# VectorE takes the square, the cast and the relu of the last feed-forward items from ScalarE

## The chip, the cores and the metric

One core of one Trainium2 chip runs the whole program. The metric is device time in microseconds (us) of one execution. Engines go by short names: PE is TensorE (PEld its weight loads), DVE is VectorE, ACT is ScalarE, POOL is GpSimd and SP is SyncE, which issues the DMAs.

## The reference

Three layers follow one another: a chunked attention (batch 4, 8 heads, 768 positions, head size 64), a soft mixture of experts, and a squared-relu feed-forward layer. The change touches only the last, whose reference is

```
h = x @ w_in                  # 3072 x 512 by 512 x 2048
r = np.maximum(h, 0.0)
g = s * (r * r) + b
out = g @ w_out               # 3072 x 2048 by 2048 x 512
```

Since `x` is itself a mixture of 32 expert outputs, the kernel computes `h` from a packed pair of small matrices and never builds `x`.

## The kernel before, in words

The first 180 us or so hold the attention and the experts. The rest is one loop over **items** (variable `n`, last loop of the kernel, from line 979 on in the profile's numbering). An item is one block of 384 tokens (`b`, 8 of them) with one slice of 128 hidden units (`f`, 16 of them), 128 items in all. The order is written out in `runs` and `items`: blocks 0 and 1 alternate for the first half of the slices (items 0 to 15), blocks 2 and 3 alternate (16 to 47), then blocks 4 to 7 follow one at a time (48 to 63, 64 to 79, 80 to 95, 96 to 111), and the second halves of blocks 0 and 1 end the program (112 to 119, 120 to 127).

One item `n` passes through these steps:

- `emit_h` (L823, PE): one matmul of 384 columns into a PSUM buffer `s`, of which there are two. I call its start T_n.
- `emit_relu` (L829, ACT), `emit_sq` (L833, ACT) and `emit_ghi` (L837, ACT): relu out of PSUM into `r`, square into `r2`, and a rounding cast into `ghi`. `r` and `r2` have two buffers each and both are printed as `r` in the profile, `ghi` and `glo` have five.
- `emit_g` (L840, DVE): the split `glo = r2 - ghi`, what the cast lost. It is issued one round later.
- `emit_o` (L875, PE), three rounds later (LA = 3): three matmuls of 512 columns of `ghi` against `w_hi`, then three of `glo` against `w_hi`. `emit_o2` (L887), one round after that: three of `ghi` against `w_lo`. All gather in three PSUM banks of the block.

When a block's last slice is done, four rounds after its `emit_h`, three **evictions** (L897, DVE) scale the three banks, add the bias and hand them to a store. With the blocks above they come in rounds 67, 83, 99, 115, 123 and 131, ahead of that round's other work on DVE.

Beside that, rounds 48 to 63 sum the weights on DVE for the bias, `colsum` makes the bias in round 64 (L850 on PE, L851 on DVE), and rounds 65 to 76 each issue one `add_bias` (L862) on POOL: a `tensor_tensor` of 128x512 with both sources in SBUF, twelve in all. They wait for the bias and for sums evicted long before, so POOL runs them back to back. The first six feed stores, the other six the evictions of rounds 123 and 131.

The whole section runs under a manual schedule: each engine takes its instructions in the order in which the program writes them, and waits only where it reads or overwrites what another wrote.

Of the kernel before, what the change touches and what calls it, by code (L numbers as in the profile page):

```python
# [14 lines left out]
ALU = mybir.AluOpType  # L15
# [19 lines left out]
def kernel(  # L35
# [11 lines left out]
    nc = tc.nc  # L47
# [11 lines left out]
    NF = w_out.shape[0] * 2  # L59
# [57 lines left out]
    with tc.manual_schedule():  # L117
# [624 lines left out]
        LA = 3  # L742
# [5 lines left out]
        def tiles(name, n, w, dt=F32):  # L748
            return [g_p.tile([128, w], dt, name=f"{name}{i}") for i in range(n)]
# [3 lines left out]
        r_g, r2_g = (tiles(x, 2, UT) for x in ("r", "r2"))  # L753
        ghi_g, glo_g = tiles("ghi", LA + 2, UT, F32R), tiles("glo", LA + 2, UT, F32R)
# [8 lines left out]
        items, place = [], {}  # L763
# [5 lines left out]
        h_t, o_t = {}, {}  # L769

        def stage_a(k):
            key = cq.get(k)
            if key:
                if key[0] == "i":
                    w = wi_src(key[1], key[2])
                else:
                    w = wt[raw_of[key]].rearrange("p (f d t) -> p f d t", f=2, t=2)[:, key[1] % 2]
                cv_act(key, k // 2 % 2, w)
# [39 lines left out]
        def emit_h(n):  # L818
            if n >= len(items):
                return  # L820
            (b, _, _), f = items[n]
            hq = psum("s", [128, UT])
            nc.tensor.matmul(out=hq, lhsT=mpack[:, 128 * f:128 * f + 128], rhs=cpack[:, b * UT:(b + 1) * UT],  # L823
                             start=True, stop=True)
            h_t[n] = hq

        def emit_relu(n):
            if n < len(items):
                nc.scalar.activation(out=r_g[n % 2], in_=h_t.pop(n), func=AF.Relu)  # L829

        def emit_sq(n):
            if n < len(items):
                nc.scalar.activation(out=r2_g[n % 2], in_=r_g[n % 2], func=AF.Square)  # L833

        def emit_ghi(n):
            if n < len(items):
                nc.scalar.copy(out=ghi_g[n % (LA + 2)], in_=r2_g[n % 2])  # L837

        def emit_g(n):
            nc.vector.tensor_tensor(out=glo_g[n % (LA + 2)], in0=r2_g[n % 2], in1=ghi_g[n % (LA + 2)].bitcast(F32),  # L840
                                    op=ALU.subtract)

        def wsum_add(i):
            if 0 < i < 2 * NF:
                a = w_hi[0].bitcast(F32) if i == 1 else wsum
                nc.vector.tensor_tensor(out=wsum, in0=a, in1=(w_hi, w_lo)[i % 2][i // 2].bitcast(F32), op=ALU.add)

        def colsum():
            c = psum("s", [128, DM])
            nc.tensor.matmul(out=c, lhsT=ones, rhs=wsum, start=True, stop=True)  # L850
            nc.vector.tensor_scalar(out=bias, in0=c, scalar1=sbt[:, 1:2], scalar2=None, op0=ALU.mult)  # L851
# [7 lines left out]
        def add_bias(i):  # L859
            j, t = divmod(i, NTU)  # L860
            os_ = os_early(j, t) if j < 2 else part[j - 2][t]
            nc.gpsimd.tensor_tensor(out=os_, in0=os_, in1=bias, op=ALU.add)  # L862
            if j < 2:
                store(2 + j, t, os_)

        def emit_o(n, parts=(0, 1)):
            r_, f = items[n]
            ghi, glo = ghi_g[n % (LA + 2)], glo_g[n % (LA + 2)]
            if f == r_[1] and 0 in parts:
                o_t[r_] = [psum(("pt", "x", "xt", "lp", "g", "g")[3 * place[r_] + t], [128, DM]) for t in range(NTU)]  # L870
            if n == len(items) - 1:
                return
            for gt in [(ghi, glo)[x] for x in parts]:
                for t in range(NTU):
                    nc.tensor.matmul(out=o_t[r_][t], lhsT=gt[:, 128 * t:128 * t + 128], rhs=w_hi[f],  # L875
                                     start=(f == r_[1] and gt is ghi), stop=False)

        def emit_o2(n):
            r_, f = items[n]
            b, f0, f1 = r_  # L880
            ghi, glo = ghi_g[n % (LA + 2)], glo_g[n % (LA + 2)]
            for t in range(NTU):
                o = o_t[r_][t]
                if n == len(items) - 1:
                    for gt in (ghi, glo):
                        nc.tensor.matmul(out=o, lhsT=gt[:, 128 * t:128 * t + 128], rhs=w_hi[f], start=False, stop=False)
                nc.tensor.matmul(out=o, lhsT=ghi[:, 128 * t:128 * t + 128], rhs=w_lo[f], start=False, stop=(f == f1 - 1))  # L887
                if f == f1 - 1:
                    if b < 4 and f0 == 0:
                        to = part[b][t] if b < 2 else os_early(b - 2, t)  # L890
                        if t == 1:
                            nc.scalar.activation(out=to, in_=o, func=AF.Copy, scale=sbt[:, 0:1])
                        else:
                            nc.vector.tensor_scalar(out=to, in0=o, scalar1=sbt[:, 0:1], scalar2=None, op0=ALU.mult)
                    else:
                        os_ = os_g[t]
                        nc.vector.scalar_tensor_tensor(out=os_, in0=o, scalar=sbt[:, 0:1], in1=part[b][t] if f0 else bias,  # L897
                                                       op0=ALU.mult, op1=ALU.add)
                        store(b, t, os_)
# [7 lines left out]
        def act(n):  # L907
            emit_relu(n)
            emit_sq(n)
            emit_ghi(n)  # L910
# [5 lines left out]
        def sums(n):  # L916
            if n in M_AT:
                emit_m(M_AT.index(n) + 1)
            if n - 1 in M_AT:
                emit_m2(M_AT.index(n - 1) + 1)  # L920

        def convert(n):
            stage_d(n, 1)
            stage_w(n)
            stages(n, 2, 3)
            stages(n - 1, 4, 5)
            stage_d(n + 1, 0)
# [7 lines left out]
        for k in range(2):  # L935
# [3 lines left out]
                  in_=sot[:, k:k + 1, :, 0:4].to_broadcast([128, 4, 4, 4]))  # L939
# [39 lines left out]
        for n in range(LA + 1, len(items) + LA + 1):  # L979
            if n > 7:  # L980
                emit_h(n)
            m = n - LA - 1
            ends = 0 <= m and items[m][1] == items[m][0][2] - 1
            late = m + 1 < len(items) and m + 1 == 2 * HF + 1
            if ends or late:
                emit_o2(m)
            if n == 2 * HF + 3:
                convert(n - 1)
            if 1 < m + 1 < len(items):
                emit_o(m + 1)  # L990
            if m > 1 and not ends and not late:
                emit_o2(m)
            if LA + 1 < n <= 7:
                emit_h(n)
            if n == 6:
                nc.vector.tensor_copy(out=soTb, in_=soT4[:, :, 0, :])
            if n <= 7:
                sums(n)
            emit_relu(n)
            emit_sq(n)  # L1000
            stage_a(n + 1)
            emit_ghi(n)
            if n > 7:
                sums(n)
            if LA + 1 < n <= len(items):
                emit_g(n - 1)

            if n != 2 * HF + 2:
                convert(n)
            if 48 <= n < 64:  # L1010
                for i in (2 * n - 96, 2 * n - 95):
                    wsum_add(i)
            if n == 64:
                colsum()
            if 65 <= n < 77:
                add_bias(n - 65)
            while n != 2 * HF + 2 and wnext[0] < len(order) and last_use.get(order[wnext[0] - NRG], -1) <= n:
                load_w(1)
# [72 lines left out]
```

## Time and profile before

| | before |
|---|---|
| median of 3 runs | 471.82 us (471.47 to 473.12) |
| the profiled execution | 471.86 us |
| its span, first to last instruction | 469.7 us |
| PE busy | 451.3 us (96%) |
| DVE busy | 290.2 us (62%) |
| ACT busy | 308.1 us (66%) |
| POOL busy | 84.2 us (18%) |
| mean granted TensorE clock | 0.991 |

The profiled execution is the one that the trace shows; 2.2 us of its time lie around the span. Busy shares are means over the whole program, so a stage is read by the view that cuts the trace into stretches. In a timeline row the first number is the start in us from the span's start and the second the length; a length in a group's row is a mean in ns.

### The profile page before, as it was taken

To read this page: it belongs to the slowest core of one execution; us is meant where nothing else is said; L and a number is where in the kernel's file an instruction comes from. 1 tells how busy PE (TensorE), PEld (TensorE's weight loads), DVE (VectorE), ACT (ScalarE), POOL (GpSimd) and SP (SyncE) were. 2 spreads that over 40 slices of the span, in tenths; PEclk is the share of its full clock that TensorE was granted. 3 is DMA by queue.
4 is the path that set the end of the run, shared out by engine and by line. 5 is a ranking of instruction groups with operands and counts; after the bars stand their busy time and mean duration, and the time that the engine had idled before them with its cause. 6 is when DMAs were issued, how large, how long until landed. Compare 5 with 4: busy or idle time off the path is not lost.

```text
span 469.7 us, 10190 instructions
## 1 busy us (share of the span) xinstructions
PE 451.3 (96%) x3960; PEld 341.5 (73%) x3960; DVE 290.2 (62%) x653; ACT 308.1 (66%) x635; POOL 84.2 (18%) x154
## 2 busy tenths in 40 slices
PE   5899999999999989999999999999999999999996
PEld 4666667565555467888787888888888888888885
DVE  6678888886465768977374988966523223224232
ACT  4466666666225469988686987666666666666660
POOL 6576556551000000000000000008600000000000
PEclk9799999999999999999999999999999999999999
DMA  8999999999999953425222000004001001001011
GB/s 299 388 391 408 405 399 405 407 387 355 422 412 401 414 216 109 163 89 180 89 91 90 2 0 0 1 0 190 13 0 69 0 1 68 0 1 67 1 67 67
DMA packets 20575, 83.03 MB, mean 177 GB/s; under 512 B 2736, under 2 KB 2864, under 8 KB 14640
## 3 DMA queue, kind: packets, MB, share of 16 engines
q1 hardware_dynamic: 20528, 82.39, 45.2%
q8 instruction: 31, 0.51, 0.4%
q14 instruction: 16, 0.13, 0.1%
HBM read 76.09 MB, written 6.29 MB: 175 GB/s over the span
## 4 chain that ended last, share of the span: by engine, by line
PE 77%; DMA 10%; DVE 7%; ACT 2%; SPq 2%; issue 1%; POOL 0%; DVEq 0%; POOLq 0%; ACTq 0%
PE g L875 12%; PE x L875 6%; PE xt L875 6%; PE pt L875 6%; PE lp L875 6%; PE g L887 6%; DMA seg<-in_w_dram 5%; PE s L823 5%; PE s L627 3%; PE pt L887 3%; PE lp L887 3%; PE x L887 3%; PE xt L887 3%; DMA vals<-in_vm_dram 3%; PE x L324 3%; PE s L284 3%
## 5 line engine op out<-in xcount | busy, mean ns | idle before, releaser
L840 DVE TENSOR_TENSOR glo<-r,ghi 128x384 fp32r<-128x384 f32 x128 | 76.7, 603 | 83.0 <-ACT ghi L837 82.9
L829 ACT ACTIVATE r<-s 128x384 f32<-128x384 f32 x128 | 62.8, 491 | 53.8 <-PE s L823 53.3
L833 ACT ACTIVATE r<-r 128x384 f32<-128x384 f32 x128 | 67.3, 526 | 7.3 <-DVE glo L840 3.0
L837 ACT CAST ghi<-r 128x384 fp32r<-128x384 f32 x128 | 65.4, 511 | 3.4
L823 PE MATMUL s<-cpack,mpack 128*128 128x384 f32 x128 | 44.1, 347 | 0.2 <-DVE mpack L816 0.2
L300 ACT ACTIVATE seg<-seg 128x384 f32<-128x384 f32 x32 | 28.8, 899 | 19.1 <-DVE seg L311 15.6
L875 PE MATMUL g<-whi,ghi 128*128 128x512 f32 x126 | 39.8, 396 | 0.3 <-DVE mpack L816 0.3
L887 PE MATMUL g<-wlo,ghi 128*128 128x512 f32 x128 | 39.6, 389 | 0.0
L875 PE MATMUL g<-whi,glo 128*128 128x512 f32 x126 | 39.3, 393 | 0.0
L862 POOL TENSOR_TENSOR keys<-keys,bias 128x512 f32<-128x512 f32 x6 | 8.4, 1428 | 161.7 <-DVE bias L851 161.7
L262 POOL TENSOR_SCALAR keys<-keys 64x416 f32<-64x416 f32 x63 | 33.6, 534 | 12.5 <-DMA keys<-in_kq_dram 7.4
L284 PE MATMUL s<-keys 128*32 128x128 f32 x768 | 29.6, 286 | 5.8 <-POOL keys L266 4.2
L324 PE MATMUL x<-vals,seg 128*32 128x128 f32 x744 | 27.8, 280 | 2.5 <-DMA vals<-in_vm_dram 1.0
L324 PEld LDWEIGHTS x<-vals,seg 128*32 128x32 f32 x744 | 20.3, 111 | 13.2 <-DVE seg L308 5.7
L823 PEld LDWEIGHTS s<-cpack,mpack 128*128 128x128 f32 x128 | 23.9, 188 | 7.2 <-issue 1.5
L887 PEld LDWEIGHTS g<-wlo,ghi 128*128 128x128 f32 x128 | 24.0, 188 | 5.1
L875 PEld LDWEIGHTS g<-whi,glo 128*128 128x128 f32 x126 | 23.6, 188 | 5.5
L284 PEld LDWEIGHTS s<-keys 128*32 128x32 f32 x768 | 19.1, 112 | 11.6 <-POOL keys L266 6.2
L318 ACT COPY seg<-pt 128x384 f32<-128x384 f32 x32 | 15.2, 476 | 18.1 <-PE pt L316 17.2
L875 PEld LDWEIGHTS g<-whi,ghi 128*128 128x128 f32 x126 | 23.7, 188 | 4.0 <-DVE mpack L816 0.8
L875 PE MATMUL xt<-whi,ghi 128*128 128x512 f32 x64 | 25.4, 397 | 0.0
L875 PE MATMUL pt<-whi,ghi 128*128 128x512 f32 x64 | 25.2, 394 | 0.0
(250 smaller groups left out, 965.3 us busy)
## 6 DMA issues: line engine op xcount, KB each, us to landing
seg<-in_w_dram SPq DMA_DIRECT2D x27, 1024.0 KB, 8.8
keys<-in_kq_dram SPq DMA_DIRECT2D x32, 396.0 KB, 7.4
vals<-in_vm_dram SPq DMA_DIRECT2D x64, 192.0 KB, 6.6
keys<-in_w_in_dram SPq DMA_DIRECT2D x5, 1024.0 KB, 5.1
keys<-in_w_out_dram SPq DMA_DIRECT2D x5, 1024.0 KB, 4.9
out_dram<-os SPq DMA_DIRECT2D x18, 256.0 KB, 2.0
vals<-in_w_in_dram SPq DMA_DIRECT2D x3, 1024.0 KB, 6.7
vals<-in_w_out_dram SPq DMA_DIRECT2D x3, 1024.0 KB, 4.8
```

The lines of the kernel that those rows point to most:

```text
L262: (nc.vector if h and u == 0 else nc.gpsimd).tensor_scalar(out=stream(kz[rows, h], 0, CH), in0=k[rows, UT * h:UT * h + (NCU + 1) * CH].rea ...
L284: nc.tensor.matmul(out=o, lhsT=qt[:, 32 * c:32 * c + 32], rhs=kz[:, :, at:at + WIN], start=True, stop=not (first or last))
L300: nc.scalar.activation(out=p_r[u], in_=sm_r[u].rearrange("p t h (a r) -> p t r (h a)", a=2), func=AF.Exp, scale=scale)
L318: nc.scalar.copy(out=pts_r[u], in_=pt)
L324: nc.tensor.matmul(out=xp[32 * r:32 * r + 32, t], lhsT=pts_r[u][:, 32 * c:32 * c + 32], rhs=vbuf[u // 2 % 2][:, u % 2, :, 64 * c:64 * c + ...
L823: nc.tensor.matmul(out=hq, lhsT=mpack[:, 128 * f:128 * f + 128], rhs=cpack[:, b * UT:(b + 1) * UT], start=True, stop=True)
L829: nc.scalar.activation(out=r_g[n % 2], in_=h_t.pop(n), func=AF.Relu)
L833: nc.scalar.activation(out=r2_g[n % 2], in_=r_g[n % 2], func=AF.Square)
L837: nc.scalar.copy(out=ghi_g[n % (LA + 2)], in_=r2_g[n % 2])
L840: nc.vector.tensor_tensor(out=glo_g[n % (LA + 2)], in0=r2_g[n % 2], in1=ghi_g[n % (LA + 2)].bitcast(F32), op=ALU.subtract)
L875: nc.tensor.matmul(out=o_t[r_][t], lhsT=gt[:, 128 * t:128 * t + 128], rhs=w_hi[f], start=(f == r_[1] and gt is ghi), stop=False)
L887: nc.tensor.matmul(out=o, lhsT=ghi[:, 128 * t:128 * t + 128], rhs=w_lo[f], start=False, stop=(f == f1 - 1))
```

## The change

From item 66 on (`DSQ = 4 * NF + 2`, with NF = 16) the square, the cast and the split are issued together on DVE, right after the relu, and ACT does none of them. From item 78 on (`DRELU = 5 * NF - 2`) the relu is a DVE instruction too, a `tensor_scalar` maximum out of PSUM, and ACT has no instruction left. `emit_g` of these items therefore moves one round earlier. The PE, POOL and SP programs are the same, instruction for instruction.

```
+        DSQ, DRELU = 4 * NF + 2, 5 * NF - 2
+
         def emit_relu(n):
-            if n < len(items):
+            if n >= len(items):
+                return
+            if n < DRELU:
                 nc.scalar.activation(out=r_g[n % 2], in_=h_t.pop(n), func=AF.Relu)
+            else:
+                nc.vector.tensor_scalar(out=r_g[n % 2], in0=h_t.pop(n), scalar1=0.0, scalar2=None, op0=ALU.max)
+            if n >= DSQ:
+                nc.vector.tensor_tensor(out=r2_g[n % 2], in0=r_g[n % 2], in1=r_g[n % 2], op=ALU.mult)
+                nc.vector.tensor_copy(out=ghi_g[n % (LA + 2)], in_=r2_g[n % 2])
+                emit_g(n)
 
         def emit_sq(n):
-            if n < len(items):
+            if n < DSQ:
                 nc.scalar.activation(out=r2_g[n % 2], in_=r_g[n % 2], func=AF.Square)
 
         def emit_ghi(n):
-            if n < len(items):
+            if n < DSQ:
                 nc.scalar.copy(out=ghi_g[n % (LA + 2)], in_=r2_g[n % 2])
@@
-            if LA + 1 < n <= len(items):
+            if LA + 1 < n <= DSQ:
                 emit_g(n - 1)
```

DVE's row from the bias of round 64 to the split of item 67, before (L851 is the bias, L840 a split, L897 an eviction):

```order
L851 TENSOR_SCALAR bias_2666<-s,cstt 128x512
L840 TENSOR_TENSOR glo_2664<-r_2653,ghi_2659 128x384
L840 TENSOR_TENSOR glo_2660<-r_2654,ghi_2655 128x384
L897 SCALAR_TENSOR_TENSOR os_2647<-pt,cstt,bias_2666 128x512
L897 SCALAR_TENSOR_TENSOR os_2648<-x,cstt,bias_2666 128x512
L897 SCALAR_TENSOR_TENSOR os_2649<-xt,cstt,bias_2666 128x512
L840 TENSOR_TENSOR glo_2661<-r_2653,ghi_2656 128x384
L840 TENSOR_TENSOR glo_2662<-r_2654,ghi_2657 128x384
```

The same stretch after the change (L861 is the bias, L837 the square, L838 the cast, L850 the split, L907 an eviction):

```order
L861 TENSOR_SCALAR bias_2666<-s,cstt 128x512
L850 TENSOR_TENSOR glo_2664<-r_2653,ghi_2659 128x384
L837 TENSOR_TENSOR r_2653<-r_2651 128x384
L838 CAST ghi_2656<-r_2653 128x384
L850 TENSOR_TENSOR glo_2661<-r_2653,ghi_2656 128x384
L850 TENSOR_TENSOR glo_2660<-r_2654,ghi_2655 128x384
L907 SCALAR_TENSOR_TENSOR os_2647<-pt,cstt,bias_2666 128x512
L907 SCALAR_TENSOR_TENSOR os_2648<-x,cstt,bias_2666 128x512
L907 SCALAR_TENSOR_TENSOR os_2649<-xt,cstt,bias_2666 128x512
L837 TENSOR_TENSOR r_2654<-r_2652 128x384
L838 CAST ghi_2657<-r_2654 128x384
L850 TENSOR_TENSOR glo_2662<-r_2654,ghi_2657 128x384
```

The split of item 65 (into `glo_2660`) now stands behind three instructions of item 66, and square, cast and split of item 67 stand behind the three evictions.

DVE's row at items 77 and 78 after the change (L835 is the relu):

```order
L837 TENSOR_TENSOR r_2654<-r_2652 128x384
L838 CAST ghi_2657<-r_2654 128x384
L850 TENSOR_TENSOR glo_2662<-r_2654,ghi_2657 128x384
L835 TENSOR_SCALAR r_2651<-s 128x384
L837 TENSOR_TENSOR r_2653<-r_2651 128x384
L838 CAST ghi_2658<-r_2653 128x384
L850 TENSOR_TENSOR glo_2663<-r_2653,ghi_2658 128x384
```

From here on DVE has four instructions for an item where it had one.

## Rows read from the trace of the kernel before

**Rows 1.** The page, busy time of PE: us, share of the span, instructions.

```profile
PE 451.3 (96%) x3960; PEld 341.5 (73%) x3960; DVE 290.2 (62%) x653; ACT 308.1 (66%) x635; POOL 84.2 (18%) x154
```

**Rows 2.** Stretches: length, then busy us and instructions of each engine, clock, DMA.

```profile
340.00:380.00 40.00, 40.00 (x181) 33.23 (x180) 11.81 (x21) 27.39 (x54) 0.00 (x0) 1.00 0.05 20
```

**Rows 3.** Timeline of one round, all engines: start us, length us, instruction, idle before.

```profile
340.12 0.33 PE L823 MATMUL s<-cpack,mpack 128*128 128x384 f32 x1
340.13 0.19 PEld L875 LDWEIGHTS lp<-whi,ghi 128*128 128x128 f32 x1
...
340.50 0.49 ACT L829 ACTIVATE r<-s 128x384 f32<-128x384 f32 x1 [0.65 <-PE s L823]
...
340.76 0.19 PEld L875 LDWEIGHTS lp<-whi,glo 128*128 128x128 f32 x1
...
342.12 0.56 DVE L840 TENSOR_TENSOR glo<-r,ghi 128x384 fp32r<-128x384 f32 x1 [1.68 <-ACT ghi L837]
...
342.37 0.33 PE L823 MATMUL s<-cpack,mpack 128*128 128x384 f32 x1
```

**Rows 4.** Timeline of PE: the hidden-layer matmuls of items 66 and 127.

```profile
319.96 0.33 PE L823 MATMUL s<-cpack,mpack 128*128 128x384 f32 x1
...
456.61 0.33 PE L823 MATMUL s<-cpack,mpack 128*128 128x384 f32 x1
```

**Rows 5.** Timeline of POOL, bias additions; the first row starts with the second of twelve.

```profile
320.23 5.37 POOL L862 TENSOR_TENSOR keys<-keys,bias 128x512 f32<-128x512 f32 x4
...
324.31 1.29 POOL L862 TENSOR_TENSOR keys<-keys,bias 128x512 f32<-128x512 f32 x1
...
325.57 1.60 POOL L862 TENSOR_TENSOR keys<-keys,bias 128x512 f32<-128x512 f32 x1
...
327.14 1.61 POOL L862 TENSOR_TENSOR part<-part,bias 128x512 f32<-128x512 f32 x1
```

**Rows 6.** Timeline of DVE beside them: two splits.

```profile
325.95 1.65 DVE L840 TENSOR_TENSOR glo<-r,ghi 128x384 fp32r<-128x384 f32 x1
327.51 1.65 DVE L840 TENSOR_TENSOR glo<-r,ghi 128x384 fp32r<-128x384 f32 x1
```

**Rows 7.** Timeline of DVE beside them: first and last eviction of block 4.

```profile
322.81 0.75 DVE L897 SCALAR_TENSOR_TENSOR os<-pt,cstt,bias 128x512 f32<-128x512 f32 x1 [2.12 <-PE pt L887]
...
324.13 0.74 DVE L897 SCALAR_TENSOR_TENSOR os<-xt,cstt,bias 128x512 f32<-128x512 f32 x1
```

**Rows 8.** Timeline at the program's start: two copies on DVE, POOL's work beside them.

```profile
4.00 0.18 DVE L231 COPY stk<-stk 128x32 f32<-128x32 f32 x1
4.09 0.83 DVE L231 COPY stk<-stk 128x32 f32<-128x32 f32 x1
...
4.00 0.57 POOL L262 TENSOR_SCALAR keys<-keys 64x416 f32<-64x416 f32 x1
```

**Rows 9.** Groups of DVE instructions of 0 to 200 us: count, busy us, mean ns, idle.

```profile
L293 DVE TENSOR_REDUCE seg<-s 128x6 f32<-128x384 f32 x32 | 17.7, 553 | 6.2 <-PE s L284 4.2 <-PE s L289 2.0
...
L951 DVE CAST whi<-seg 128x512 fp32r<-128x512 f32 x1 | 0.4, 428 | 0.0
...
L996 DVE CAST seg<-keys 128x128 bf16<-128x128 f32 x1 | 0.2, 219 | 0.0
```

**Rows 10.** Timeline of DVE, three in a row without idle time between.

```profile
264.44 0.55 DVE L840 TENSOR_TENSOR glo<-r,ghi 128x384 fp32r<-128x384 f32 x1
264.91 0.69 DVE L789 TENSOR_TENSOR seg<-seg,whi 128x512 f32<-128x512 f32 x1
265.63 0.69 DVE L791 TENSOR_TENSOR wlo<-seg 128x512 fp32r<-128x512 f32 x1
```

**Rows 11.** Stretches near the program's start, columns as in rows 2.

```profile
3.66:10.48 6.82, 3.03 (x68) 2.17 (x66) 4.34 (x11) 2.02 (x3) 4.32 (x10) 1.00 0.95 352
10.48:17.31 6.83, 5.62 (x80) 3.93 (x81) 3.93 (x12) 2.67 (x4) 2.59 (x6) 0.50 1.01 379
```

## The prediction, made before the changed kernel ran

> **What bounds the kernel now.** I read the page's busy times first: PE is busy for 451.3 of 469.7 us [rows 1], and DVE's 62% and ACT's 66% are means over stages that differ. So next the stretches: from 340 to 380 us PE works all 40.00 of 40.00 us at clock 1.00, DVE 11.81, ACT 27.39, POOL nothing [rows 2]. PE is the bound of the last section, and DVE has room. Then one round in the timeline [rows 3]: the hidden-layer matmul starts at 340.12 and again at 342.37, a round of 2.24 us (61 rounds from item 66 at 319.96 to item 127 at 456.61 [rows 4] give the same). ACT's relu starts 0.38 us after T_n, the split ends at 2.56. PE asks for `ghi` of the item three rounds back (its weight load) at T_n + 0.01 and for `glo` at T_n + 0.64. So the `glo` that is ready at T_n + 2.56 is wanted at T_n + 6.72 + 0.64 = T_n + 7.36: 4.8 us of slack, and a delay on DVE or ACT below that is hidden.
>
> The last view is the one that decides: POOL beside DVE. From 320.23 us POOL runs the second of its twelve bias additions, just when item 66 begins. Left alone one takes 1.25 us (324.31 to 325.57), beside a split the next starts 1.57 us later (325.57 to 327.14) [rows 5]. The splits beside them take 1.65 us instead of 0.55, and start 1.56 apart [rows 6, 10]: one split gets through per POOL instruction, after waiting for it to end. The evictions do not suffer: 0.75 us each, 0.66 apart, in the middle of POOL's work [rows 7]; their large source is in PSUM. At the program's start a small DVE copy from SBUF to SBUF took 0.83 us beside POOL's 0.57 us instruction, the one just ahead of it 0.18 [rows 8]. So DVE instructions with two SBUF sources, and copies within SBUF, wait for POOL. Before the change DVE has one of these per item (the split), 1.57 us out of 2.24: hidden. The change makes it three.
>
> **The change part by part.**
>
> *Taken from ACT:* three instructions per item. ACT's chain was inside the slack, so this gives nothing.
>
> *Prices on DVE, alone.* Square: a `tensor_tensor` of 128x384 with two SBUF sources, like the split, 0.55 us [rows 10]. Cast: 0.428 us for 512 elements, 0.219 for 128 [rows 9], by the line between them 0.36 for 384. Relu: the nearest read of 128x384 from PSUM took 0.553 [rows 9]. An instruction that needs the one before starts 0.03 after its end (264.91 + 0.69 to 265.63), one that does not starts 0.47 after a split's start [rows 10]. So items 66 to 77 cost 0.58 + 0.39 + 0.47 = 1.44 us each on DVE, items from 78 on 1.44 + 0.58 = 2.02, both under the 2.24 of a round.
>
> *From 78 on: hidden.* An eviction adds 3 x 0.66 us and starts 0.61 after T_n (322.81 against 322.20) where the relu would start at 0.38: the item is 2.2 us late. 0.22 us per round wins this back in ten rounds of the sixteen to the next. At round 123, eight after 115, 0.4 is left and the lateness reaches 2.4. What ends first is the PSUM buffer: T_n+2 needs the relu of n done, 4.48 us after T_n; at 2.4 late it is done at 0.38 + 2.4 + 0.56 = 3.3. I cost this part at nothing; its cover is these 1.1 us.
>
> *Items 66 to 69, beside POOL: this is the sum.* I walk DVE's queue as the change orders it. Each waiting instruction ends 1.57 us after the one before it, as in [rows 5, 6] (a cast, 0.2 shorter, 1.37). The relu of item 66 ends on ACT at 319.96 + 0.38 + 0.49 = 320.83; POOL's second addition holds until 320.23 + 1.25 or so, 321.5. Square 66 ends at 322.0, cast 66 at 323.4, split 66 at 325.0, and the split of item 65, which now stands behind these three, at 326.6 to 326.7. Then three evictions, 2.0 us, during which POOL runs its sixth addition alone and is in the seventh until about 329.0. Square 67 ends at 329.5, cast 67 at 330.9, split 67 at 332.5 to 332.7, square 68 at 334.2, cast 68 at 335.6, split 68 at 337.2 to 337.4. That uses POOL's twelve; from then an item takes DVE 1.44.
>
> What PE makes of it, each due time from rows 3 and T_n = 319.96 + 2.24 (n - 66):
> - Round 68 wants `glo` of 65 at 324.44 + 0.64 = 325.1. It is there at 326.7: **1.6 late**.
> - Round 69 (item 66) finds all there.
> - Round 70 starts 1.6 late, at 330.5. `ghi` of 67 comes at 330.9, 0.4 late; `glo`, due at 331.6, at 332.7: **1.5 more** in all.
> - Round 71 starts at 334.3. `ghi` of 68 comes at 335.6, 1.3 late; `glo`, due at 336.3, at 337.4: **2.4 more**.
> - Round 72 starts at 338.9; item 69, at 1.44 after 337.4, is there. After that DVE gains 0.8 us per round and the slack is back before item 78.
>
> Sum 1.6 + 1.5 + 2.4 = 5.5 us, which PE never wins back, as it has no idle time. The profiled execution's 471.86 us (0.04 above the median of the runs shown) becomes **477.4 us**. The unknown in it is the cast beside POOL. Lower bound: it does not wait (0.39 us), the case below with 2.2 us. Upper bound: a copy waits out two POOL instructions, as the 0.83 us in rows 8 could be read; each cast of 66 to 68 would then end 1.25 later, but POOL would be done sooner and the walk ends at 338.0 instead of 337.4, 6.2 us in all. I take the single wait, since that is what the 1.65 us splits of the same size and engine state show.
>
> **The rivals.**
>
> *The cast does not wait for POOL; square and split do.* Two waits per item. Same walk: split 65 ends at 325.1, just in time; squares and splits of 67 to 70 then come every 1.57 us and reach PE 0.6, 0.9 and 0.4 to 0.7 us late in rounds 71 to 73: about 2.2 us, **474.1**. For it: that case had no cast of this size beside POOL. Against: the 0.83 us copy.
>
> *Only the split waits (not slower).* The square reads one tensor twice; if that counts as a single source, and the cast passes as well, one DVE instruction per item waits, as before. Square and cast then run 0.97 us inside a POOL instruction and an item takes 1.57 us. It decides at 2.24 us per item: below that nothing reaches PE, **471.9**. Against: a split reads two tensors of the same kind in the same way, and nothing in the rows tells the two apart.
>
> *POOL starts only when the waiting DVE instruction is over.* Then the pitch of the waits is 1.25 + 0.55 = 1.8 us, and some nine pitches in the walk make it 2 us longer: **479.4**. Against: the measured 1.57 [rows 5, 6]. This is how the Trainium skill tells it (SBUF — State Buffer, section Who interferes with whom): the shared port pair is held for the whole instruction and the other side blocks fully. The measurement decides, and here it speaks for an earlier release; the sum stays at 1.57.
>
> *DVE becomes the bound from 78 on.* Late by 2.2 us after each eviction, it must win back 2 us in 16 rounds, so the point is 2.11 us per item; I have 2.02. If the cast ran at the pace of the split (0.55 instead of 0.36) an item took 2.2 and four evictions of 2 us would outrun the 3.5 us of slack by some 5 us on top of 5.5: **482.3**. Against: 0.428 us for 512 elements [rows 9] is well under the 0.69 of a two-source instruction of that size [rows 10].
>
> *The clock falls.* In the walk PE stands still for about 3.9 of the 8.4 us from 330.5 on. Near the start PE was busy for 3.03 of 6.82 us, and the next 6.83 us ran at granted clock 0.50, the lower level, 1.2 GHz [rows 11]. One such stretch costs half of 6.83, 3.4 us: **480.8**. Against: the idle time here falls into pieces of 0.4 to 1.3 us between full matmuls.
>
> **How the numbers follow.** A measurement of this kernel can tell about 0.5% from no change: 2.4 us, so 469.5 to 474.2 counts as the same. The walk as forecast, 475.5 to 479: 0.62. The longer pitch: 0.04. The cast passes, 474.1, on the border: 0.12. Only the split waits: 0.06. DVE bound: 0.08. Clock: 0.06. Faster by a mechanism that I do not see: 0.02. Slower: 0.62 + 0.04 + 0.08 + 0.06 = 0.80 and a sixth of 0.12, 0.82; the rest of the 0.12 and the 0.06 make the same, 0.16; faster 0.02. The range goes from 473.7, just under the passing cast, to 482.0, above the clock's case; what it leaves out is the hidden case and most of the DVE-bound one.
>
> **What would show it.** Right: squares, casts and splits of 0.9 to 1.7 us between 320 and 337 us, POOL's additions 1.57 apart until about 337; PE idle before L885 (the `emit_o` line of the changed kernel) with DVE as releaser, once near 325 and twice between 330 and 338; rounds of 2.24 us with PE full after that, and DVE busy for 36 to 38 of 40 us. Wrong: casts of 0.36 us beside POOL (474.1), PE without idle time there (471.9), rounds longer than 2.24 us after 360 us or waits of PE for the relu (DVE bound), or a stretch at clock 0.50.

## The result and the profile after

| | before | after |
|---|---|---|
| median of 6 runs each | 472.5 us | 477.38 us (476.3 to 479.33) |
| ratio, 95% interval | | 1.0107 [1.0078, 1.0136] |
| the profiled execution | 471.86 us | 479.33 us |
| its span | 469.7 us | 477.3 us |
| item 66 to item 127, start to start | 136.65 us | 143.03 us |

The change makes the kernel slower by 1.1%, some 5 us. The profiled execution of the change is 7.5 us above that of before, and not all of it belongs to the change: item 66 already starts at 321.19 instead of 319.96 us [rows 4], 1.2 us later, in a part of the program that the change does not touch. From trace to trace of this study that start lies anywhere between 318.6 and 323.8 us. So the traces are compared from item 66 to item 127, where nothing of that counts. These are the two rows of the kernel after:

```profile
321.19 0.33 PE L823 MATMUL s<-cpack,mpack 128*128 128x384 f32 x1
...
464.22 0.33 PE L823 MATMUL s<-cpack,mpack 128*128 128x384 f32 x1
```

61 rounds take 143.03 us, 6.4 us more than before. The row of busy times shows the work that moved: DVE from 290.2 to 374.0 us, ACT from 308.1 to 219.1, PE and POOL as before but for some 2 us of PE [rows 1].

```profile
PE 453.4 (95%) x3960; PEld 342.1 (72%) x3960; DVE 374.0 (78%) x827; ACT 219.1 (46%) x461; POOL 84.1 (18%) x154
```

The stretches say where the time went (columns as in rows 2):

```profile
330.00:340.00 10.00, 7.62 (x28) 5.01 (x27) 9.62 (x11) 1.47 (x3) 7.47 (x6) 0.91 0.40 154
340.00:350.00 10.00, 10.00 (x43) 8.25 (x42) 7.85 (x17) 1.97 (x4) 0.00 (x0) 0.91 0.00 1
...
360.00:400.00 40.00, 40.00 (x180) 33.23 (x179) 37.30 (x75) 0.00 (x0) 0.00 (x0) 1.00 0.05 20
```

From 330 to 340 us PE works 7.62 of 10 us while DVE and POOL are busy. From 360 us on PE is full again, with 180 matmuls in 40 us as before (181 in [rows 2]), although DVE now has 37.30 of 40 us instead of 11.81. The loss lies in a few rounds.

DVE's timeline in those rounds, items 65 to 68 (the square is L837, the cast L838, the split L850; the row at 326.04 is the split of item 65). The three evictions, left out here, run between 327.59 and 329.65:

```profile
322.09 1.09 DVE L837 TENSOR_TENSOR r<-r 128x384 f32<-128x384 f32 x1 [1.74 <-ACT r L833]
323.28 1.27 DVE L838 CAST ghi<-r 128x384 fp32r<-128x384 f32 x1
324.58 1.53 DVE L850 TENSOR_TENSOR glo<-r,ghi 128x384 fp32r<-128x384 f32 x1
326.04 1.63 DVE L850 TENSOR_TENSOR glo<-r,ghi 128x384 fp32r<-128x384 f32 x1
...
329.57 0.92 DVE L837 TENSOR_TENSOR r<-r 128x384 f32<-128x384 f32 x1
330.52 1.34 DVE L838 CAST ghi<-r 128x384 fp32r<-128x384 f32 x1
331.90 1.52 DVE L850 TENSOR_TENSOR glo<-r,ghi 128x384 fp32r<-128x384 f32 x1
333.34 1.64 DVE L837 TENSOR_TENSOR r<-r 128x384 f32<-128x384 f32 x1
335.01 1.31 DVE L838 CAST ghi<-r 128x384 fp32r<-128x384 f32 x1
336.36 1.52 DVE L850 TENSOR_TENSOR glo<-r,ghi 128x384 fp32r<-128x384 f32 x1
...
339.32 0.55 DVE L837 TENSOR_TENSOR r<-r 128x384 f32<-128x384 f32 x1
```

But for the evictions these are ten instructions in a row, of 0.9 to 1.6 us each; the last row, after POOL is done at 337.47, is the same square in 0.55. POOL beside the first of them:

```profile
322.71 1.62 POOL L872 TENSOR_TENSOR keys<-keys,bias 128x512 f32<-128x512 f32 x1
324.28 1.42 POOL L872 TENSOR_TENSOR keys<-keys,bias 128x512 f32<-128x512 f32 x1
325.66 1.59 POOL L872 TENSOR_TENSOR keys<-keys,bias 128x512 f32<-128x512 f32 x1
```

From start to start they are 1.57 us apart beside a `tensor_tensor` and 1.38 beside a cast. One DVE instruction passes between two of POOL's. And PE waits for what comes late. These are its rows with idle time, in rounds 68, 70 and 71, and the start of round 72:

```profile
327.73 0.50 PE L885 MATMUL lp<-whi,glo 128*128 128x512 f32 x1 [1.02 <-DVE glo L850]
...
333.47 0.50 PE L885 MATMUL lp<-whi,glo 128*128 128x512 f32 x1 [0.59 <-DVE glo L850]
...
336.38 0.50 PE L885 MATMUL lp<-whi,ghi 128*128 128x512 f32 x1 [1.07 <-DVE ghi L838]
...
337.94 0.50 PE L885 MATMUL lp<-whi,glo 128*128 128x512 f32 x1 [0.59 <-DVE glo L850]
...
340.37 0.52 PE L823 MATMUL s<-cpack,mpack 128*128 128x384 f32 x1
```

By the starts of L823, rounds 68, 70, 71 and 72 are 1.30, 1.27, 3.16 and 0.63 us longer than 2.24; all others are as before. In the last of these rows the matmul takes 0.52 us instead of 0.33: after the waits the granted clock stood at 0.50, the lower level, for 3.41 us from 338.29 on. That is the 0.91 in two rows of the stretches.

```profile
338.29:341.70 3.41, 3.41 (x10) 2.73 (x9) 3.03 (x8) 0.98 (x2) 0.00 (x0) 0.50 0.00 0
```

### The profile page after: what moved, and what is told of

The parts are those of the page before. It is cut to its first block, busy times and chain, and to the rows that moved or that the text cites. A ratio compares the mean times of both kernels' runs of the same rounds, so it can differ in the third digit from the quotient of the medians.

```text
span 477.3 us, 10090 instructions
## 1 busy us (share of the span) xinstructions
PE 453.4 (95%) x3960; PEld 342.1 (72%) x3960; DVE 374.0 (78%) x827; ACT 219.1 (46%) x461; POOL 84.1 (18%) x154
## 4 chain that ended last, share of the span: by engine, by line
PE 75%; DVE 10%; DMA 6%; ACT 2%; POOL 2%; issue 2%; SPq 2%; DVEq 0%; POOLq 0%; ACTq 0%
PE g L885 11%; PE xt L885 6%; PE x L885 6%; PE pt L885 6%; PE g L897 6%; PE lp L885 6%; PE s L823 4%; DMA seg<-in_w_dram 3%; PE s L627 3%; PE s L284 3%; PE pt L897 3%; DMA vals<-in_vm_dram 3%; PE xt L897 3%; PE x L897 3%; PE lp L897 3%; PE x L324 3%
## 5 line engine op out<-in xcount | busy, mean ns | idle before, releaser
L850 DVE TENSOR_TENSOR glo<-r,ghi 128x384 fp32r<-128x384 f32 x128 | 75.1, 587 | 7.9 <-ACT ghi L847 5.7
L833 ACT ACTIVATE r<-s 128x384 f32<-128x384 f32 x78 | 38.2, 490 | 41.2 <-PE s L823 27.8
L823 PE MATMUL s<-cpack,mpack 128*128 128x384 f32 x128 | 44.3, 348 | 0.2 <-DVE mpack L816 0.2
L837 DVE TENSOR_TENSOR r<-r 128x384 f32<-128x384 f32 x62 | 36.5, 589 | 6.1 <-ACT r L833 4.4
L897 PE MATMUL g<-wlo,ghi 128*128 128x512 f32 x128 | 40.1, 393 | 0.0
L843 ACT ACTIVATE r<-r 128x384 f32<-128x384 f32 x66 | 34.7, 526 | 4.1 <-DVE glo L850 2.0
L262 POOL TENSOR_SCALAR keys<-keys 64x416 f32<-64x416 f32 x63 | 33.6, 533 | 14.1 <-DVE seg L296 3.3
L847 ACT CAST ghi<-r 128x384 fp32r<-128x384 f32 x66 | 33.6, 509 | 1.4
L823 PEld LDWEIGHTS s<-cpack,mpack 128*128 128x128 f32 x128 | 24.1, 189 | 7.2 <-issue 1.5
L835 DVE TENSOR_SCALAR r<-s 128x384 f32<-128x384 f32 x50 | 27.6, 552 | 1.1
L897 PEld LDWEIGHTS g<-wlo,ghi 128*128 128x128 f32 x128 | 24.3, 190 | 5.3
L838 DVE CAST ghi<-r 128x384 fp32r<-128x384 f32 x62 | 25.2, 406 | 2.8
L885 PE MATMUL lp<-whi,glo 128*128 128x512 f32 x63 | 24.8, 394 | 2.2 <-DVE glo L850 2.2
```

The source lines that it names most:

```text
L262: (nc.vector if h and u == 0 else nc.gpsimd).tensor_scalar(out=stream(kz[rows, h], 0, CH), in0=k[rows, UT * h:UT * h + (NCU + 1) * CH].rea ...
L837: nc.vector.tensor_tensor(out=r2_g[n % 2], in0=r_g[n % 2], in1=r_g[n % 2], op=ALU.mult)
```

## The experiments

The theory: the loss is DVE waiting for POOL's bias additions, three times per item, until PE wants an item that is not there. The rival: DVE has too much to do or its chain is too long, with or without POOL. The measure beside the ratio is the time from item 66 to item 127 in the profile; the start of the program moves the total by more than the effects that are sought. The time around the span differs too, 1.8 to 2.0 us in the kernels with an edit and 2.1 to 2.2 in the kernel before, so a ratio comes out up to 0.3 us lower than the section.

| kernel | item 66 to 127, us | rounds longer than 2.24, us | ratio to before, 95% interval |
|---|---|---|---|
| before | 136.65 | none | 1 |
| the change | 143.03 | 68: 1.30, 70: 1.27, 71: 3.16, 72: 0.63 | 1.0107 [1.0078, 1.0136] |
| from item 78 on only | 136.64 | none | 0.9989 [0.9975, 1.0004] |
| bias additions on DVE | 136.64 | none | 1.0029 [1.0015, 1.0044] |
| six of twelve additions on POOL | 137.93 | 68: 1.29 | 1.0028 [1.0011, 1.0045] |
| square on ACT up to item 77 | 137.55 | 71: 0.21, 72: 0.71 | 1.0007 [0.9988, 1.0026] |
| relu on ACT to the end | 141.44 | 68: 1.30, 70: 1.26, 71: 2.22 | 1.0077 [1.0062, 1.0092] |
| from item 70 on | 137.78 | 72: 1.14 | 1.0016 [0.9997, 1.0035] |
| split of item 65 first | 141.80 | 70: 1.34, 71: 3.19, 72: 0.61 | 1.0099 [1.0069, 1.0128] |
| extra DVE instruction | 139.12 | 116: 0.84, 117: 0.10, 124: 1.39, 125: 0.13 | 1.0039 [1.0025, 1.0054] |

### Only the last part

```
-        DSQ, DRELU = 4 * NF + 2, 5 * NF - 2
+        DSQ, DRELU = 5 * NF - 2, 5 * NF - 2
```

> Only the last part of the change: square, cast, split and relu on DVE from item 78 on, where POOL has finished its bias additions. If the loss is DVE waiting for POOL (theory), none is left: item 127 starts 136.7 us after item 66, as before (143.0 in the changed kernel), and the time is that of before, ratio 1.000. If the loss is DVE's load or the longer chain of one engine (rival), most items that carry it are still there (50 of 62) and at least 4 us of the 5 to 6 remain, ratio 1.008 or more.

Every round has its old length. Its stretch from 360 us on is as busy on DVE as that of the changed kernel:

```profile
360.00:400.00 40.00, 40.00 (x180) 33.22 (x180) 37.51 (x76) 0.00 (x0) 0.00 (x0) 1.00 0.10 40
```

So 50 items with all their elementwise work on DVE cost nothing, and the rival falls for this part. Nor do they gain: the interval of the ratio holds 1, and PE was full before.

### The bias additions on DVE

```
-            nc.gpsimd.tensor_tensor(out=os_, in0=os_, in1=bias, op=ALU.add)
+            nc.vector.tensor_tensor(out=os_, in0=os_, in1=bias, op=ALU.add)
```

> The change whole, but the twelve bias additions run on DVE, one per round 65 to 76, so POOL is still while DVE has MORE to do (12 x 0.67 us). Theory: no wait for POOL, DVE at 1.44 + 0.67 = 2.11 us of a 2.24 us round, nothing reaches PE: item 127 starts 136.7 us after item 66, ratio 1.000. Rival (DVE's own load): slower than the changed kernel by up to 8 us, ratio 1.011 to 1.03.

DVE does twelve instructions more in rounds 65 to 76, which hold all those that were long, POOL stands still, and no round is long. From 313 to 345 us, with item 66 at 320.99:

```profile
313.00:330.00 17.00, 17.00 (x76) 13.78 (x75) 12.07 (x23) 6.69 (x14) 0.00 (x0) 1.00 0.23 90
330.00:345.00 15.00, 15.00 (x69) 12.46 (x68) 14.04 (x30) 3.44 (x7) 0.00 (x0) 1.00 0.15 58
```

This is the run that decides: the whole change, with more on DVE, loses nothing in its rounds as soon as POOL does not work beside it. Yet the ratio is 1.0029 and not 1.000. The time is at the end: from item 127 to the end of the span 14.7 us pass, in the other nine kernels of the table 13.1. The last experiment comes back to this.

### Six of twelve on POOL

```
-            nc.gpsimd.tensor_tensor(out=os_, in0=os_, in1=bias, op=ALU.add)
+            (nc.gpsimd if i < 6 else nc.vector).tensor_tensor(out=os_, in0=os_, in1=bias, op=ALU.add)
```

> The change whole, but of the twelve bias additions only the first six stay on POOL, the last six go to DVE in rounds 71 to 76. Theory: the late split of item 65 stays (1.6 to 1.7 us in round 68), the waits of items 67 and 68 go: item 127 starts 138.4 us after item 66, ratio 1.003 to 1.004. Rival (DVE's own load): no less than the changed kernel, 143 us or more.

Round 68 is 1.29 us longer, and rounds 70 and 71 have no wait: the theory holds to the round. The size is 0.3 to 0.4 us under the expected 1.6 to 1.7.

### Square on ACT up to item 77

```
-                nc.vector.tensor_tensor(out=r2_g[n % 2], in0=r_g[n % 2], in1=r_g[n % 2], op=ALU.mult)
+                if n < DRELU:
+                    nc.scalar.activation(out=r2_g[n % 2], in_=r_g[n % 2], func=AF.Square)
+                else:
+                    nc.vector.tensor_tensor(out=r2_g[n % 2], in0=r_g[n % 2], in1=r_g[n % 2], op=ALU.mult)
```

> The square of items 66 to 77 goes back to ACT, so an item has two waits for POOL (cast and split) and not three. Theory, cast waits like the split: 1.5 to 2 us are left, item 127 starts 138.3 to 138.7 us after item 66, ratio 1.003 to 1.005. If the cast does not count: nothing is left, 136.7. If the number of waits does not matter: 142 to 143.

0.9 us are left, under the expected 1.5 to 2, and the ratio of 1.0007 is under the expected 1.003 to 1.005. Two casts of this kernel (L841), the first ahead of POOL, the second behind it:

```profile
325.27 0.36 DVE L841 CAST ghi<-r 128x384 fp32r<-128x384 f32 x1 [2.29 <-ACT r L838]
...
332.89 1.45 DVE L841 CAST ghi<-r 128x384 fp32r<-128x384 f32 x1
```

The cast waits for POOL like the split, but the first one found POOL just between two additions (one ends at 325.38) and did not wait; the expectation counts two waits in every item. That the number of waits per item sets the loss holds (three: 4.8 us without the clock's part, two: 0.9, one, as before: none); the step from two to three is steeper than I had worked out.

### Relu on ACT to the end

```
-        DSQ, DRELU = 4 * NF + 2, 5 * NF - 2
+        DSQ, DRELU = 4 * NF + 2, len(items)
```

> The change without its last step: square, cast and split on DVE from item 66, but the relu stays on ACT to the end. Theory: the relu on DVE costs and gives nothing, the waits beside POOL remain: item 127 starts 142.4 us after item 66 (143.0 if the clock falls for 3.4 us in round 71 again), ratio 1.009 to 1.014. Rival (DVE's load from 78 on has a part in the loss): 141 us or less.

The waits of rounds 68 and 70 are the same to 0.01 us, round 71 is 2.22 us longer instead of 3.16, round 72 not at all. The total of 141.44 stands between the two forecasts, 142.4 and 141 or less, so this run alone does not tell them apart. What is missing is not the relu's: the clock stayed at full level here, and the changed kernel with its relu on DVE takes 141.42 us when the clock stays up (its second profile, below).

```profile
330.00:340.00 10.00, 7.75 (x31) 5.55 (x32) 9.52 (x13) 1.47 (x3) 5.47 (x4) 1.00 0.20 76
340.00:350.00 10.00, 10.00 (x47) 8.27 (x46) 8.04 (x17) 2.46 (x5) 0.00 (x0) 1.00 0.00 1
```

So the waits alone cost 4.8 us, and the clock's part of the changed kernel's first profile is 143.03 - 141.44 = 1.6 us. The ratio is a miss: 1.0077 is under the expected 1.009 to 1.014 and makes 3.6 us (2.9 to 4.3) from four runs; the start of the program, which differs by 5 us between traces, may hide the rest, but this was not tried.

### From item 70 on

```
-        DSQ, DRELU = 4 * NF + 2, 5 * NF - 2
+        DSQ, DRELU = 4 * NF + 6, 5 * NF - 2
```

> DVE takes square, cast and split from item 70 on instead of 66, when POOL has four or five of its twelve additions left and the evictions of round 67 are over. Theory: only items 70 and 71 meet POOL, 0.5 to 1.5 us reach PE: item 127 starts 137.1 to 138.1 us after item 66, ratio 1.001 to 1.004. Rival (every item with its work on DVE costs a share): 58 of 62 items remain, 142 us.

1.14 us, in one round, as expected: 58 of the 62 items still have their work on DVE, and the loss has shrunk to a quarter of 4.8.

### The split of item 65 first

```
             if n >= DSQ:
+                if n == DSQ:
+                    emit_g(n - 1)
...
-            if LA + 1 < n <= DSQ:
+            if LA + 1 < n < DSQ:
```

> The change with one pair of instructions exchanged: the split of item 65 stands ahead of item 66's square instead of behind its split. Theory: round 68 is not late any more, but the number of waits in the queue is the same, so items 67 and 68 are later by what round 68 had hidden: 4.5 to 5 us in all, item 127 starts 141.2 to 141.7 us after item 66 (0.6 more if the clock falls), ratio 1.008 to 1.012. Rival (the exchanged order is the cause, POOL is not): 137 us, ratio 1.00.

Round 68 is not late any more, rounds 70 and 71 are, and the clock fell here too (3.41 us at 0.50, from 336.59 on). The total of 141.80, near the expected one, includes that part; if it is the 1.6 us measured above, the waits cost 3.6 us, not 4.5 to 5. The order of the queue is worth more than expected but is not the cause.

### One more DVE instruction per item

```
-        DSQ, DRELU = 4 * NF + 2, 5 * NF - 2
+        DSQ, DRELU = 5 * NF - 2, 5 * NF - 2
...
                 emit_g(n)
+                nc.vector.tensor_scalar(out=ones, in0=ones, scalar1=1.0, scalar2=None, op0=ALU.mult)
```

> As the run with only the last part (DVE from item 78 on), with one more small DVE instruction per item from 78 on (128x128, SBUF to SBUF, about 0.15 to 0.2 us of DVE's time, on a tile that nobody reads any more). It measures the cover of the last part: by the prices of the prediction an item then takes 2.17 to 2.22 us of a 2.24 us round, past the point of 2.11 at which the evictions can't be won back, so 2.5 to 4.7 us reach PE in rounds 99 to 127, PE waiting for the relu: item 127 starts 139 to 141.4 us after item 66, ratio 1.005 to 1.010. If DVE has more room than that, 136.6 and ratio 1.00.

2.48 us, just at the lower end; the ratio of 1.0039 is under the expected 1.005 to 1.010. PE waits for the relu, and only after the evictions of rounds 115 and 123:

```profile
433.72 0.45 PE L823 MATMUL s<-cpack,mpack 128*128 128x384 f32 x1 [0.68 <-DVE r L835]
```

The extra instruction lasts 0.22 us, and the next one starts 0.13 after its start. By the starts of the relu right behind an eviction an item takes DVE 2.18 us, against 2.05 without the extra instruction, so a round of 2.24 us wins back 0.06 us and not 0.19. The relu is 2.2 us late after round 83 in both kernels, and in this one 3.3 after round 99 and 4.3 after round 115, where PE waits. This is how near the last part of the change stands to its edge: 0.13 us more per item, and it costs.

### The change a second time

The changed kernel itself, unedited.

> The changed kernel a second time, for its clock alone. The three waits of PE must be the same to some hundredths (1.30, 1.27 and 2.22 us in rounds 68, 70 and 71 as the run with the relu on ACT has them). If the lower clock level after them belongs to the waits, it is there again and round 71 and 72 are 0.9 and 0.6 us longer (143.0 us from item 66 to 127); if it depends on when the waits fall, it may be missing as with the relu on ACT (141.4 us).

141.42 us from item 66 to 127, with 1.32, 1.27 and 2.21 us in rounds 68, 70 and 71 and none in 72. The waits come back to 0.02 us, the lower clock does not: the stretch from 330 to 340 has 1.00 with the same busy time of PE, 7.61 against 7.62 us.

```profile
330.00:340.00 10.00, 7.61 (x31) 5.17 (x30) 9.70 (x10) 1.48 (x3) 7.57 (x6) 1.00 0.42 158
```

So one and the same kernel had 3.41 us at the lower level after its waits in one profile and none in the other. Of four profiles with waits this long (the change twice, the relu on ACT, the split first) two have it. What decides is open. This profile comes from another chip than the experiments above, and for the first profile of the change the chip is not on record, so the chip is not excluded either.

### The bias additions on DVE a second time

The same kernel as above with that name, unedited.

> The kernel with the bias additions on DVE a second time, for its end alone. In its first profile item 127 started 136.64 us after item 66, as before, but 14.7 us passed from there to the end of the span where the kernel before has 13.1. If that belongs to the kernel it is there again (14.2 or more); if it was chance, 13.1.

136.64 us again, and 14.6 us from item 127 to the end: the longer end belongs to the kernel. The DMA queues from 458 us on (packets, MB, share) show what is there in addition:

```profile
q1 hardware_dynamic: 432, 0.79, 14.6%
q14 instruction: 2, 0.02, 0.3%
```

These are two loads of instructions, of 8 KB each. One starts at 468.5, among the packets of the last store, whose landing is 1.0 us later after item 127's start than in the other kernels; the second starts at 471.7, when the span of 471.3 us is over. In the second profile of the change the stretch from 463 us on has the store's packets alone:

```profile
q1 hardware_dynamic: 432, 0.79, 15.6%
```

In the traces of the kernel before, of six additions on POOL and of the relu on ACT such a load starts 14.1 to 14.8 us after item 127's start, past the end of the span, and in the remaining kernels of the table none is traced after item 127's start. That the load makes the end longer is argued from this, not tried. The end is 1.5 to 1.6 us longer, which is about the 1.4 us of the ratio 1.0029.

## Why the prediction was right

Forecast 477.4 us, measured 477.38; that the numbers agree to 0.02 us is luck. The forecast added 5.5 us to 471.86; measured was a loss of 4.88 on a median of before of 472.5. The waits were 0.7 us smaller than forecast, the base was 0.6 us higher, and the clock, for which the sum had no term, added 1.6 us in some profiles.

**The mechanism** held in each step. DVE instructions with two SBUF sources and the cast take 0.9 to 1.6 us beside POOL, one per POOL addition; the evictions out of PSUM do not wait (0.74 us each). The square, which reads one tensor twice, waits like the split, so the rival in which only the split waits falls. The cast takes 1.27 to 1.34 us beside POOL and 0.36 without; the rival in which it passes falls with that. The additions on DVE remove the loss from the rounds, which shows that it is POOL and not DVE's load.

**The pitch** was right: 1.56 us between the ends of two waiting `tensor_tensor`s (326.12 and 327.67), 1.37 where a cast comes next (323.17 to 324.55). If POOL started only when the waiting DVE instruction is over it would be 1.25 + 0.55 = 1.8 us; that rival falls. The Trainium skill (SBUF — State Buffer, section Who interferes with whom) says that whoever issues first gets the shared port pair for the whole instruction; the 1.56 us here speak for an earlier release. Its list of the DVE instructions that contend with POOL (two SBUF inputs; copies and casts in a two-port mode) agrees with the squares, splits and casts here.

**The terms of the sum** were each a little too large: 1.6 forecast and 1.30 measured in round 68, 1.5 and 1.27 in round 70, 2.4 and 2.22 in round 71, together 5.5 and 4.8 us. The walk was late: measured from item 66's start, the split of item 65 ends at 6.48 us where the walk had 6.7, the cast of item 67 at 10.67 and not 10.9, the split of item 68 at 16.69 and not 17.4. Ends were rounded up, or the later of two was taken (332.7, 337.4), and the errors added, since each instruction waits for the one before it.

**The clock** came in as the rival said, with a smaller price: 1.6 us for 3.41 us at the lower level, where I had 3.4 us for 6.83. It came in two of four profiles, and I had given it 0.06. What I had held against it, that the idle time falls into pieces of 0.4 to 1.3 us, did not keep the clock up in those two: the pieces of the first were 0.12 to 1.07 us. The prediction also names a stretch at 0.50 as a sign of being wrong; the sign came, and the sum is short of it by a term. The range held all six times of the changed kernel.

**From 78 on** nothing was lost, as costed. An item takes DVE 2.05 us back to back where the sum had 2.02, and the relu is 2.2 us late after an eviction and 2.65 at round 123, where it had 2.2 and 2.4. The prices were right: square 0.558 us, cast 0.360, relu 0.552, split 0.558 in the changed kernel, against 0.55, 0.36, 0.553 and 0.55:

```profile
L850 DVE TENSOR_TENSOR glo<-r,ghi 128x384 fp32r<-128x384 f32 x55 | 30.7, 558 | 1.9
L837 DVE TENSOR_TENSOR r<-r 128x384 f32<-128x384 f32 x54 | 30.1, 558 | 4.2 <-ACT r L833 2.5
L835 DVE TENSOR_SCALAR r<-s 128x384 f32<-128x384 f32 x50 | 27.6, 552 | 1.1
L838 DVE CAST ghi<-r 128x384 fp32r<-128x384 f32 x55 | 19.8, 360 | 2.3
```

The run with one more instruction shows the edge about where the prediction had put it: PE did not wait with the relu 3.3 us late and did at 4.3; the sum had 2.4 and 1.1 of cover. The waits are where it said (the relu), though they begin one eviction later than the expectation said.

## What to carry to other kernels

Before work goes to DVE, look at what POOL does at that hour: a cast of 0.36 us alone cost 1.3 us here and a `tensor_tensor` of 0.55 us 0.9 to 1.6, and the count of those that meet POOL, not DVE's busy share, decided. Such a move can be free for 50 items and cost 5 us through four, so read it from the timeline of the rounds where two engines meet, and move either the start of the change or the other engine's work. And walk the waits in a chain with unrounded numbers: here the roundings of ten ends made most of an error of 0.7 us in 5.5.

## What the runs showed of the hardware

The same kernel with the same waits of PE (idle pieces of 1.08 us at most, three rounds longer by 4.8 us together) ran once with 3.41 us at granted clock 0.50 after them and once without. A change in one part of a program can also go with a load of instructions at another place: with twelve instructions taken from POOL and given to DVE, one such load fell among the packets of the last store in both profiles, and the end took 14.6 to 14.7 us instead of 13.1.
